# Seven half-size block products in place of eight in a dense expert's first GEMM, one batch at a time

## The chip, the cores and the metric

The kernel runs on one core of a Trainium2 chip. The metric is the device time of one execution in microseconds (us). TensorE (PE) multiplies, VectorE (DVE), ScalarE (ACT) and GpSimd (POOL) do the rest, SyncE (SP) issues most transfers. The engines run on their own, each in its own fixed order, and wait for one another by semaphores.

## The reference

Attention whose mask keeps pairs with equal hash codes, then a mixture of 8 dense experts in which every token goes through every expert, then one in which each token goes to 2 of 8 experts. B = 2 batches, H = 8 heads, S = 768, head size 64; N = B S = 1536 tokens, D = 512, F = 1024, E = 8, all in float32.

```
x = attention(q, k, v, proj)                    # N x D
P = exp(x @ w_gate - max)
for _ in range(8):                              # Sinkhorn
    P /= P.sum(1, keepdims=True) + 1e-09
    P /= P.sum(0, keepdims=True) + 1e-09
    P *= N / E
for e in range(E):                              # dense experts
    h = np.maximum(x @ w1[e], 0.0)              # first GEMM,  D -> F
    out += P[:, e:e + 1] * (h @ w2[e])          # second GEMM, F -> D
...
noisy = out @ w_gate2 + log1p(exp(out @ w_noise)) * noise
# top 2 of 8, softmax over the two, then for each expert e and its tokens m:
out2[m] += top2_w[m] * (np.maximum(out[m] @ v1[e], 0.0) @ v2[e])
```

## The kernel before

Every large product is done three times in a reduced float32 format: an operand is split into a high part (a copy that rounds) and a low part (value minus high part), and high·high, high·low and low·high are added in one PSUM bank.

*Attention* (lines 130 to 386). Its steps are issued by a table of times in units of half a head. The last ones of a head pair are the fold steps: POOL adds two halves and writes the high and low parts of x, `xh` and `xl` (L327, L53, L331); the last pair of a batch goes through PE instead (`fold_last`).

*Dense experts* (`moe1`). Sixteen steps u: expert u // 2, half of F u % 2. In each, three tiles t of 512 tokens. For a tile, GEMM1 makes four banks `ph` (128 units of F by 512 tokens) of 4 × 3 matmuls 128x512 (L507 to L509); ACT writes the high part `hh` (relu, L512), DVE the low part `hl` (L513). Then GEMM2 makes four banks `py` (128 tokens by 512) of 4 × 3 matmuls (L520 to L522), and DVE adds them, times the expert's weight, to `acc` (L530). The weights come in pieces of 512x512, 1 MB each (`Pieces.fetch`, L400), and are split in four chunks by ACT (L418) and DVE (L419) a step ahead. Each piece is fetched once.

*Gate and routing.* `moe1_gate` gets the gate's logits in 24 matmuls and runs Sinkhorn (a chain of small DVE operations with one small matmul each round, L481) while the first dense step runs. In the last dense step, as each token tile of `acc` is finished, `Route.tile` writes it out and transposes it, and `Route.span` computes the choice for some tiles together (`SPANS`), with a PE chain of its own (L593, L594, L599).

*Sparse experts* (`moe2_round`). 416 slots for each expert, filled by a gather (L755) and transposed by PE (L767). The first expert takes its tokens in two units of `CAPH` = 256 slots: its first `JH` = 5 token tiles, whose gather starts before the dense stage ends, and the rest.

*What sets the order.* A scheduler orders the instructions of each engine ahead of time from its own model of durations, under the program's data dependencies, pool sizes and priorities. PSUM has 8 banks: three for `ph`, three for `py`, two for small things (`PsPools`). The instructions of GEMM1 (L507 on) are put by it into the attention's tail where x is ready.

Of the kernel before, what the change touches and what calls it, by code (L numbers as in the profile page):

```python
# [18 lines left out]
P = 128  # L19
NC = S // P           # query/key tiles per batch  # L20
NJ = B * NC           # token tiles
N = B * S
# [10 lines left out]
assert CAP + 4 * CAP2 == N and 0 <= 2 * CAPH - CAP <= CAPH and JH in SPANS  # L33


# when the steps of the attention are issued, in halves of a head
# [5 lines left out]
SUMS = [1.52, 2.12, 2.38, 1.85, 2.31, 2.53]  # L42
EARLY = [4, 7, 9, "g", "g", "g"]
WARM = [26, -0.0, 10]
FIRST = [27.07, 27.44, 27.71, 31.92]
# [10 lines left out]
def build_consts(nc, pool, tmp, proj):  # L56
# [13 lines left out]
    # routing tables  # L70
# [10 lines left out]
    # a token's row in the scratch, 128 j + p, and in the output  # L81
# [8 lines left out]
def attention_consts(nc, pool, c):  # L90
    # [I; I] placed in columns 0..63 or 64..127
# [9 lines left out]
    # what 0 counts as in each row of the codes, and the rows' scale  # L101
# [14 lines left out]
def projections(nc, c):  # L116
    """High and low parts, of a head pair, negated and as they are: columns 0..11 and 32..43 for queries, 64 more for keys."""
# [12 lines left out]
def attention(ctx, tc, c, q, k, v, xh, xl, others=()):  # L130
# [40 lines left out]
    def split_half(st, nm, hf):  # L171
        """High and low parts, transposed; the queries times -1/8."""
# [12 lines left out]
    def stack(st, nm):  # L185
        """One product has high and low queries over high keys twice, the other high queries over low keys, and the codes."""
# [4 lines left out]
        if nm == "q":  # L191
            # [hi0 lo0] [hi1 lo1]; [hi0 .] [hi1 .]
# [5 lines left out]
        else:  # L198
            # [hi0 hi0] [hi1 hi1]; [lo0 .] [lo1 .]
# [24 lines left out]
            # 1 where positive, else -1: 0 is not positive  # L224
# [26 lines left out]
    # ---- per half of a head: 3 query tiles  # L251
    def score(st, x, hf, i, un):
# [5 lines left out]
        if st.first and x == 0:  # L258
            # its parts as they are, before any move
# [9 lines left out]
        # the scores are negated  # L269
# [6 lines left out]
    def norm(un):  # L276
        """e / (sum + 1e-9), or 1 / S in a row without a matching key."""
# [44 lines left out]
    def fold(st, hf, step):  # L322
        """The products with the high values and those with the low ones, added; a pair of heads stacked."""
        xs = slice(st.b * S + hf * 384, st.b * S + hf * 384 + 384)
        a, b = (t[:, cols(hf)] for t in st.ab)
        if step == 0:
            tc.keep_in_program_order(nc.gpsimd.tensor_add(a, a, b))  # L327
        elif step == 1:
            copy_on_pool(nc, xh[:, st.pair, xs], a)
        else:  # L330
            tc.keep_in_program_order(nc.gpsimd.tensor_sub(xl[:, st.pair, xs], a, xh[:, st.pair, xs].bitcast(F32)))  # L331

    def fold_last(st, hf):
        xs = slice(st.b * S + hf * 384, st.b * S + hf * 384 + 384)
# [4 lines left out]
        nc.scalar.activation(xh[:, st.pair, xs], px, AF.Copy)  # L339
        nc.vector.tensor_sub(xl[:, st.pair, xs], px, xh[:, st.pair, xs].bitcast(F32))  # L340
# [3 lines left out]
    for m in range(B * H // 2):  # L344
# [36 lines left out]
        else:  # L381
            for hf in range(2):
                for i in range(3):
                    at(t0 + 3 + VALUE[-1] + 0.01 + SUMS[3 * hf + i], fold, st, hf, i)
# [5 lines left out]
class Pieces:  # L390
    """The weights as 512 x 512 pieces, loaded and split into high and low parts ahead of use."""

    def __init__(self, nc, rawpool, pools, srcs):
        self.nc, self.rawpool, self.pools, self.srcs = nc, rawpool, pools, srcs
        self.raw, self.part = {}, {}

    def fetch(self, i):
        if i < len(self.srcs) and i not in self.raw:
            r = self.rawpool.tile([P, 4, FH], F32, name="wraw", tag="wraw")
            self.nc.sync.dma_start(r, self.srcs[i][0].rearrange("(c p) f -> p c f", p=P))  # L400
            self.raw[i] = r

    def chunk(self, i, k):
        return (slice(None), slice(None), slice(k * P, (k + 1) * P)) if self.srcs[i][1] else (slice(None), k)

    def high(self, i):
# [590 lines left out]
```

## Time and profile before

| | |
|---|---|
| median of 3 runs | 1736.48 us (1736.42 to 1738.51) |
| profiled execution, span | 1738.8 us |
| instructions | 21681 |
| PE busy | 1699.5 us (98%) |
| DVE busy | 770.6 us (44%) |
| ACT busy | 559.3 us (32%) |
| POOL busy | 267.7 us (15%) |

The profiled execution's own time is its span, from the first to the last instruction; no other time of it is recorded. It lies 2.3 us above the median of the runs. The attention takes about the first 290 us, the dense experts go to about 1374, the sparse ones to the end. Busy time counts an engine while it works on an instruction; matmuls overlap in PE's pipeline, so the distance between two starts says what one of them costs, and its own duration is longer.

### The profile page before, as it was taken

Reading aid. Unit: us, or ns where it says so; the run is one execution under the profiler, and the core shown is the slowest. Engines: PE = TensorE matmul, PEld = TensorE weight load, DVE = VectorE, ACT = ScalarE, POOL = GpSimd, SP = SyncE. Lnnn points to the kernel's source line nnn. Section 1 sums busy time; section 2 is a strip of 40 time slices with the busy share of each in tenths; the row PEclk is TensorE's granted clock in tenths of the full one; section 3 lists DMA queues with packets and bytes.
Section 4 is the critical chain, followed back from the end, with each engine's and each line's share of the span. In section 5 each row is a group of like instructions: output and inputs, shape, how many; then the busy total and the mean of one; then the engine's idle time right before and its main releaser. Section 6 shows DMA issues by size and latency. Waiting matters only on the chain. (4 is left out here: it accounts for less than half of the span.)

```text
span 1738.8 us, 21681 instructions
## 1 busy us (share of the span) xinstructions
PE 1699.5 (98%) x8504; PEld 1451.1 (83%) x8504; DVE 770.6 (44%) x1611; ACT 559.3 (32%) x1129; POOL 267.7 (15%) x282
## 2 busy tenths in 40 slices
PE   9999999999999999999999999999999999999995
PEld 6988897788888888888888888888888899999995
DVE  4998995353233233333332333332333765443340
ACT  3878884322021121121121121121111344444431
POOL 3676762002000000000000000000000022322221
PEclk7999999999999999999999999999999999999997
DMA  6755421211010010010010010110101235555531
GB/s 144 193 137 135 96 68 27 75 47 33 16 49 25 25 49 25 25 49 25 25 49 25 25 49 5 45 49 1 49 25 67 92 94 155 156 149 140 145 89 22
DMA packets 87581, 117.21 MB, mean 67 GB/s; under 512 B 33784, under 2 KB 41976, under 8 KB 87472
## 3 DMA queue, kind: packets, MB, share of 16 engines
q1 hardware_dynamic: 80240, 101.60, 19.9%
q0 software_dynamic: 7232, 14.15, 4.4%
q8 instruction: 69, 1.13, 0.3%
q14 instruction: 40, 0.33, 0.1%
HBM read 83.77 MB, written 13.35 MB: 56 GB/s over the span
## 5 line engine op out<-in xcount | busy, mean ns | idle before, releaser
L512 ACT ACTIVATE hh<-ph 128x512 fp32r<-128x512 f32 x192 | 114.0, 596 | 753.0 <-PE ph L509 753.0
L509 PE MATMUL ph<-xh,wlo 128*128 128x512 f32 x768 | 303.6, 395 | 0.0
L508 PE MATMUL ph<-xl,whi 128*128 128x512 f32 x768 | 303.1, 395 | 0.0
L507 PE MATMUL ph<-xh,whi 128*128 128x512 f32 x768 | 302.1, 394 | 0.0
L521 PE MATMUL py<-wlo,hh 128*128 128x512 f32 x768 | 296.1, 395 | 0.0
L520 PE MATMUL py<-whi,hh 128*128 128x512 f32 x768 | 292.0, 396 | 0.0
L522 PE MATMUL py<-whi,hl 128*128 128x512 f32 x768 | 288.9, 395 | 0.0
L513 DVE SCALAR_TENSOR_TENSOR hl<-ph,hh 128x512 fp32r<-128x512 f32 x192 | 132.4, 691 | 326.0 <-ACT hh L512 326.0
L530 DVE SCALAR_TENSOR_TENSOR acc<-py,Pm,acc 128x512 f32<-128x512 f32 x168 | 121.2, 748 | 296.2 <-PE py L522 296.1
L419 DVE TENSOR_TENSOR wlo<-wraw,whi 128x512 fp32r<-128x512 f32 x252 | 159.0, 688 | 109.1 <-ACT whi L418 106.7
L755 POOL DMA_INDIRECT xg<-x2d,idx x32 | 35.3, 1104 | 1013.4 <-DVE idx L751 949.1
L418 ACT ACTIVATE whi<-wraw 128x512 fp32r<-128x512 f32 x252 | 138.4, 620 | 126.3 <-PE py L522 32.2
L507 PEld LDWEIGHTS ph<-xh,whi 128*128 128x128 f32 x768 | 144.9, 189 | 33.8 <-ACT e L272 0.2
L520 PEld LDWEIGHTS py<-whi,hh 128*128 128x128 f32 x768 | 144.3, 188 | 34.4
L522 PEld LDWEIGHTS py<-whi,hl 128*128 128x128 f32 x768 | 144.2, 188 | 34.4
L521 PEld LDWEIGHTS py<-wlo,hh 128*128 128x128 f32 x768 | 144.2, 188 | 34.3
L508 PEld LDWEIGHTS ph<-xl,whi 128*128 128x128 f32 x768 | 144.2, 188 | 33.4
L509 PEld LDWEIGHTS ph<-xh,wlo 128*128 128x128 f32 x768 | 144.2, 188 | 33.1
L294 DVE TENSOR_TENSOR el<-pe,eh 128x384 fp32r<-128x384 f32 x192 | 101.0, 548 | 12.5 <-ACT eh L293 12.1
L285 POOL TENSOR_SCALAR e<-e,f,g 128x768 f32<-128x768 f32 x96 | 93.3, 985 | 54.8 <-DVE f L283 45.7
L290 PE MATMUL pe<-ident,e 128*128 128x128 f32 x576 | 93.5, 275 | 6.3 <-DVE el L294 5.2
L270 DVE TENSOR_REDUCE mn<-pS 128x1 f32<-128x768 f32 x96 | 91.1, 949 | 18.0 <-PE pS L268 18.0
(253 smaller groups left out, 2367.1 us busy)
## 6 DMA issues: line engine op xcount, KB each, us to landing
wraw<-in_moe_w_dram SPq DMA_DIRECT2D x64, 1024.0 KB
ab<-pvf SPq DMA_DIRECT2D x28, 192.0 KB
raw_q<-in_q_dram SPq DMA_DIRECT2D x16, 192.0 KB
raw_k<-in_k_dram SPq DMA_DIRECT2D x16, 192.0 KB
raw_v<-in_v_dram SPq DMA_DIRECT2D x8, 384.0 KB
ka<-kh SPq DMA_DIRECT2D x16, 192.0 KB
out_dram<-zero SPq DMA_DIRECT2D x1, 3072.0 KB
x2d<-acc SPq DMA_DIRECT2D x12, 256.0 KB
```

What stands on the lines that cost most here:

```text
L294: nc.vector.tensor_sub(el, pt, eh.bitcast(F32))
L418: nc.scalar.activation(hi[ix], r[ix], AF.Copy)
L419: nc.vector.tensor_sub(lo[ix], r[ix], hi[ix].bitcast(F32))
L507: nc.tensor.matmul(ph, w1h[:, k, fs], xh[:, k, ts], start=(k == 0), stop=False)
L508: nc.tensor.matmul(ph, w1h[:, k, fs], xl[:, k, ts], start=False, stop=False)
L509: nc.tensor.matmul(ph, w1l[:, k, fs], xh[:, k, ts], start=False, stop=(k == DC - 1))
L512: nc.scalar.activation(hh, ph, AF.Relu)
L513: nc.vector.scalar_tensor_tensor(hl, ph, 0.0, hh.bitcast(F32), op0=ALU.max, op1=ALU.subtract)
L520: nc.tensor.matmul(py, a, w2h[:, k, :], start=(k == 0), stop=False)
L521: nc.tensor.matmul(py, a, w2l[:, k, :], start=False, stop=False)
L522: nc.tensor.matmul(py, b, w2h[:, k, :], start=False, stop=(k == 3))
L530: nc.vector.scalar_tensor_tensor(acc[:, j, :], py, Pm[:, j, e:e + 1], acc[:, j, :], op0=ALU.mult, op1=ALU.add)
```

## The change

The dense stage takes one batch (768 tokens) at a time, in 32 steps n: batch n // 16, expert, half of F. In a step, GEMM1 is x (768 x 512) times w1 (512 x 512). Both are cut into 2 x 2 blocks (384 tokens by 256 of D; 256 of D by 256 of F), and the four result blocks are made from seven products of sums of blocks (Winograd's form of Strassen's scheme) in place of eight products of blocks. The sums of x's blocks are made once per batch (`left`), those of w1's blocks once per step, on POOL (`source`), and split into high and low parts as all operands are (`right`). A product is 2 × 2 × 3 matmuls 128x384, 84 in a step. Four of the seven add to a bank that holds an earlier product. The sums over products are taken from PSUM by ACT and DVE (`hidden`); then GEMM2 goes over the batch's six token tiles (`output`), its matmuls as before, 72 in a step.

Around it: the weights are fetched for either batch, in pieces of half a MB and chunks of 128 rows; the folds of the attention write x itself, in float32 (one POOL addition); gate and routing use 48 float32 matmuls each, straight from x, in place of split operands; routing takes three token tiles together and does batch 0 in the middle of the stage; JH is 6 and CAPH 224; PSUM has four banks for GEMM1 and two for GEMM2.

```diff
-JH, CAPH = 5, 256
-SPANS = {2: 0, 5: 2, 9: 5, 12: 9}
+JH, CAPH = 6, 224
+HT = S // 2
+FP = F // 4
...
-            copy_on_pool(nc, xh[:, st.pair, xs], a)
-            tc.keep_in_program_order(nc.gpsimd.tensor_sub(xl[:, st.pair, xs], a, xh[:, st.pair, xs].bitcast(F32)))
+        tc.keep_in_program_order(nc.gpsimd.tensor_add(xr[st.b][:, st.pair, cols(hf)], a, b))
...
+        src = self.srcs[key].rearrange("(h c p) f -> h p c f", p=P, c=2)
+        for h in range(2):
+            r = self.rawpool.tile([P, 2, FH], F32, name="wraw", tag="wraw")
+            self.nc.sync.dma_start(r, src[h])
...
+    for j in range(NJ):
         for k in range(DC):
-            nc.tensor.matmul(pg, wga[:, 0, k, :], xh[:, k, ts], start=(k == 0), stop=False)
-            nc.tensor.matmul(pg, wga[:, 1, k, :], xl[:, k, ts], start=False, stop=(k == DC - 1))
+            nc.tensor.matmul(pl[:, j], xr[j // NC][:, k, (j % NC) * P:(j % NC + 1) * P], wg[:, k], start=(k == 0), stop=(k == DC - 1))
...
+class Dense:
+    def source(self, n, i):
...
+        if i in (0, 2, 6):
+            return (b11, b21, b22)[i // 2 if i < 6 else 2]
+        def t(m, x, y):
...
+                nc.gpsimd.tensor_sub(o, x, y)
...
+        t1 = t(1, b12, b11)
+        if i == 4:
+            return t1
+        if i == 3:
+            return t(3, b22, b12)
+        t2 = t(2, b22, t1)
+        return t2 if i == 1 else t(4, b21, t2)
+    def right(self, n, i, on_pool=False):
...
+            nc.scalar.activation(hi, src, AF.Copy)
+            nc.vector.tensor_sub(lo, src, hi.bitcast(F32))
+    def left(self, b, xo, tmp):
...
+            nc.vector.tensor_add(s[0], x21[:, k], x22[:, k])
+            nc.vector.tensor_sub(s[1], s[0], x11[:, k])
+            nc.gpsimd.tensor_sub(s[2], x11[:, k], x21[:, k])
+            nc.gpsimd.tensor_sub(s[3], x12[:, k], s[1])
...
+    def hidden(self, n, hp, tmp, after):
...
+        for i in range(7):
+            at = "xyxyzyz"[i]
...
+                for k in range(2):
+                    nc.tensor.matmul(ph, wh[:, k, fs], xh[:, k], start=(i in (0, 1, 4) and k == 0), stop=False, skip_group_check=True)
+                    nc.tensor.matmul(ph, wh[:, k, fs], xl[:, k], start=False, stop=False, skip_group_check=True)
+                    nc.tensor.matmul(ph, wl[:, k, fs], xh[:, k], start=False, stop=(k == 1), skip_group_check=True)
+            for s in range(2):
+                ph, su = banks[s][at], sums[s]
+                if i == 0:
...
+                    nc.scalar.activation(su["p1"], ph, AF.Copy)
+                elif i in (1, 3):
...
+                    nc.vector.tensor_add(su[i], ph, su["p1"])
+                elif i == 2:
+                    keep(s, 0, 0, ph)
+                else:
+                    v, (t, f) = {4: (su[3], (1, 1)), 5: (su["p1"], (1, 0)), 6: (su[1], (0, 1))}[i]
+                    nc.vector.tensor_add(v, ph, v)
+                    keep(s, t, f, v)
...
-    for u in range(2 * E):
+    dense.left(0, xo, tmp)
+    for n in range(steps):
...
+            if i < 4:
+                wt.split(w2(n), i)
+            if i == 1:
+                wt.fetch(w1(n + 1))
...
+        dense.hidden(n, hp, tmp, after)
+        if n == 0:
+            moe1_gate(nc, c, gp, ps, wg, xr, Pm)
+        if last and b == 0:
+            dense.left(1, xo, tmp)
+        for m in range(6):
+            t, i = 1 - m // 3, m % 3
+            j, a = dense.output(n, t, i, acc, Pm)
...
+            if n + 1 < steps:
+                dense.right(n + 1, m)
...
-                      for t, b in (("h", 3), ("y", 3), ("g", 2))}
+                      for t, b in (("h", 4), ("y", 2), ("g", 2))}
```

`keep` takes relu's high part on ACT and its low part on DVE. Line numbers of the kernel after are its own.

PE's order at the end of the attention, before: the last scores (`pS`) and transposes (`pe`), and behind them GEMM1 (`ph`).

```order
L268 MATMUL pS<-kb,qb 128x384
L290 MATMUL pe<-ident,e 128x128 x15
L507 MATMUL ph<-xh,whi 128x512
L508 MATMUL ph<-xl,whi 128x512
L509 MATMUL ph<-xh,wlo_3522 128x512
```

After, at the end of the attention; `px` of L330 and L331 is the last fold, `px` and `py` of L561 on are banks of products 0 and 1.

```order
L330 MATMUL px<-pvs,fold 128x384
L331 MATMUL px<-pvs,fold 128x384
L561 MATMUL px<-xh_4143,wh 128x384 x2
L561 MATMUL py<-xh_4145,wh 128x384 x2
L562 MATMUL px<-xl_4144,wh 128x384
L563 MATMUL px<-xh_4143,wl 128x384
```

The first matmuls of GEMM1 stand between the attention's last transposes before, and behind its last fold after.

DVE's order in the middle of a dense step, before: low parts of hidden units (`hl`), of weights (`wlo`), and accumulations (`acc`).

```order
L513 SCALAR_TENSOR_TENSOR hl_7420<-ph_7406,hh_7419 128x512
L513 SCALAR_TENSOR_TENSOR hl_7437<-ph_7423,hh_7436 128x512
L419 TENSOR_TENSOR wlo_7638<-wraw_7251,whi_7637 128x4x128 x4
L513 SCALAR_TENSOR_TENSOR hl_7454<-ph_7440,hh_7453 128x512
L530 SCALAR_TENSOR_TENSOR acc_4164<-py_7457,Pm_4171,acc_4164 128x512
```

After, in a step, from product 4 on: sums over a bank (`u`, `p1`), low parts of hidden units (`hl`), of w2 (`wl` of L412) and of w1's blocks of the next step (`wl` of L506).

```order
L576 TENSOR_TENSOR u_6159<-pz_6167,u_6159 128x384
L576 TENSOR_TENSOR u_6161<-pz_6174,u_6161 128x384
L412 TENSOR_TENSOR wl_6428<-wraw_6357,wh_6427 128x512
L576 TENSOR_TENSOR p1_6089<-py_6097,p1_6089 128x384
L548 SCALAR_TENSOR_TENSOR hl_6183<-u_6159,hh_6182 128x384
L548 SCALAR_TENSOR_TENSOR hl_6188<-u_6161,hh_6187 128x384
L576 TENSOR_TENSOR p1_6091<-py_6104,p1_6091 128x384
L412 TENSOR_TENSOR wl_6448<-wraw_6357,wh_6447 128x512
L576 TENSOR_TENSOR u_6111<-pz_6167,u_6111 128x384
L548 SCALAR_TENSOR_TENSOR hl_6205<-p1_6089,hh_6204 128x384
L576 TENSOR_TENSOR u_6113<-pz_6174,u_6113 128x384
L506 TENSOR_TENSOR wl_6594<-wt_6591,wh_6593 128x512
```

A bank now passes through a sum before its parts are taken, and a weight's low part stands between the sums.

## Rows read from the trace of the kernel before

**Rows 1.** The page: busy time of each engine; PE's granted clock in 40 slices

```profile
PE 1699.5 (98%) x8504; PEld 1451.1 (83%) x8504; DVE 770.6 (44%) x1611; ACT 559.3 (32%) x1129; POOL 267.7 (15%) x282
...
PEclk7999999999999999999999999999999999999997
```

**Rows 2.** Stretches of the dense stage: busy time (instructions) of engines, clock, DMA

```profile
480.00:680.00 200.00, 200.00 (x860) 161.36 (x860) 64.14 (x96) 33.21 (x59) 0.00 (x0) 1.00 0.10 32
...
1080.00:1280.00 200.00, 200.00 (x861) 161.61 (x860) 64.71 (x96) 33.98 (x60) 0.00 (x0) 1.00 0.10 32
```

**Rows 3.** PE in time: start, duration, line, operation; 384 columns wide

```profile
273.13 0.33 PE L302 MATMUL pv<-eh,vv 128*128 128x384 f32 x1
...
275.03 0.34 PE L303 MATMUL pv<-el,vv 128*128 128x384 f32 x1
```

**Rows 4.** PE in time, sparse stage, 416 columns wide

```profile
1441.09 0.35 PE L841 MATMUL ph<-exh,whi 128*128 128x416 f32 x1
...
1447.52 0.35 PE L842 MATMUL ph<-exl,whi 128*128 128x416 f32 x1
```

**Rows 5.** Groups: busy time, mean ns of one, and idle time before

```profile
L419 DVE TENSOR_TENSOR wlo<-wraw,whi 128x512 fp32r<-128x512 f32 x252 | 159.0, 688 | 109.1 <-ACT whi L418 106.7 <-PE ph L509 2.4
...
L418 ACT ACTIVATE whi<-wraw 128x512 fp32r<-128x512 f32 x252 | 138.4, 620 | 126.3 <-PE py L522 32.2 <-PE ph L508 31.3 <-DMA wraw<-in_moe_w_dram 27.4
L513 DVE SCALAR_TENSOR_TENSOR hl<-ph,hh 128x512 fp32r<-128x512 f32 x192 | 132.4, 691 | 326.0 <-ACT hh L512 326.0
L530 DVE SCALAR_TENSOR_TENSOR acc<-py,Pm,acc 128x512 f32<-128x512 f32 x168 | 121.2, 748 | 296.2 <-PE py L522 296.1
...
L294 DVE TENSOR_TENSOR el<-pe,eh 128x384 fp32r<-128x384 f32 x192 | 101.0, 548 | 12.5 <-ACT eh L293 12.1
...
L293 ACT ACTIVATE eh<-pe 128x384 fp32r<-128x384 f32 x192 | 88.3, 492 | 27.0 <-PE pe L290 19.5 <-PE pv L302 6.7 <-ACT eh L293 0.3
```

**Rows 6.** Groups on POOL

```profile
L430 POOL TENSOR_TENSOR wlo<-wraw,whi 128x512 fp32r<-128x512 f32 x4 | 5.1, 1298 | 0.0
```

**Rows 7.** DVE and POOL in time at 266; all of L294, shortest, median, longest

```profile
266.46 0.97 DVE L281 TENSOR_SCALAR sm<-sm 128x3 f32<-128x3 f32 x1 [0.57 <-ACT e L272]
...
266.40 1.98 POOL L331 TENSOR_TENSOR xl<-ab,xh 128x384 fp32r<-128x384 f32 x2
...
L294 DVE TENSOR_TENSOR el<-pe,eh x192: 521/549/559, 42.1 to 284.4; 128x384 fp32r<-128x384 f32 x192
```

**Rows 8.** PE in time, from the first expert's unit 0 to unit 1

```profile
1404.46 0.60 PE L767 MATMUL pxt<-ident,xg 128*128 128x128 f32 x4
...
1406.82 0.48 PE L841 MATMUL ph<-exh,whi 128*128 128x256 f32 x2
```

**Rows 9.** PE in time, around a Sinkhorn matmul

```profile
387.78 0.28 PE L481 MATMUL pc<-cs,ones 128*128 128x8 f32 x2
387.92 0.48 PE L507 MATMUL ph<-xh,whi 128*128 128x512 f32 x1
388.23 0.39 PE L508 MATMUL ph<-xl,whi 128*128 128x512 f32 x1
```

**Rows 10.** Groups on PE: a small matmul of the routing

```profile
L599 PE MATMUL pl<-fold,lt 32*128 32x16 f32 x24 | 3.3, 261 | 0.5 <-ACT lt L596 0.5
```

**Rows 11.** The end of the attention as one stretch

```profile
260.00:300.00 40.00, 37.66 (x197) 31.50 (x197) 24.57 (x54) 18.91 (x43) 10.77 (x12) 1.00 0.03 3
```

**Rows 12.** PE in time, sparse stage, with the idle time before

```profile
1584.69 0.72 PE L876 MATMUL py<-ehh,whi 128*128 128x416 f32 x1 [2.04 <-ACT ehh L846]
```

**Rows 13.** A stretch of the dense stage with one weight piece's transfer

```profile
565.00:572.00 7.00, 7.00 (x31) 5.65 (x31) 1.77 (x3) 1.20 (x2) 0.00 (x0) 1.00 0.51 150
```

**Rows 14.** PE in time at two waits, and the stretch behind them

```profile
1373.84 1.06 PE L599 MATMUL pl<-fold,lt 32*128 32x16 f32 x8 [0.51 <-ACT lt L596]
...
1376.18 0.94 PE L767 MATMUL pxt<-ident,xg 128*128 128x128 f32 x4 [0.70 <-DVE d L610]
...
1376.00:1380.00 4.00, 3.82 (x15) 3.67 (x16) 3.04 (x15) 0.85 (x3) 0.00 (x0) 0.57 0.64 245
```

More of the change, by code (lines that the diff above doesn't have):

```diff
@@ L127, in projections, with attention @@
             nc.vector.tensor_copy(c.hw[nm][hs, :, at:at + 12], p2[hs].bitcast(F32))
-def attention(ctx, tc, c, q, k, v, xh, xl, others=()):
+def attention(ctx, tc, c, q, k, v, xr, others=()):
     nc = tc.nc
@@ L382, in attention @@
             for hf in range(2):
-                for i in range(3):
-                    at(t0 + 3 + VALUE[-1] + 0.01 + SUMS[3 * hf + i], fold, st, hf, i)
+                at(t0 + 3 + VALUE[-1] + 0.01 + SUMS[hf], fold, st, hf)
     for _, _, fn, a in sorted(steps, key=lambda s_: s_[:2]):
@@ L489, in moe1 @@
+def moe1(ctx, tc, c, dense, wt, ps, wg, xa, xr, route, first, ep):
     nc = tc.nc
-    hp = ctx.enter_context(tc.tile_pool(name="m_h", bufs=6, side="right"))
-    gp = ctx.enter_context(tc.tile_pool(name="m_g", bufs=1, side="right"))
+    xo = ctx.enter_context(tc.tile_pool(name="xo", bufs=1, side="right", reuse_waits="tile"))
+    tmp = ctx.enter_context(tc.tile_pool(name="m_t", bufs=6, side="right", reuse_waits="tile"))
+    hp = ctx.enter_context(tc.tile_pool(name="m_h", bufs=8, side="right", reuse_waits="tile"))
+    gp = ctx.enter_context(tc.tile_pool(name="m_g", bufs=1, side="right", reuse_waits="tile"))
@@ new lines, in moe1, with w1, w2, after @@
+    steps = 4 * E
+    def w1(n):
+        return "w1", n // 2 % E, n % 2, n // (2 * E)
+    def w2(n):
+        return "w2", n // 2 % E, n % 2, n // (2 * E)
+    dense.left(0, xo, tmp)
+    for i in range(3, 7):
+        dense.right(0, i)
+    for n in range(steps):
+        b, u = n // (2 * E), n % (2 * E)
+        wt.fetch(w2(n))
+        def after(i):
+            if i < 4:
+                wt.split(w2(n), i)
+            if i == 1:
+                wt.fetch(w1(n + 1))
+            if n == steps - 1 and i > 2:
+                wt.split(("v1", 0, 0), i - 3, i < 6)
+        dense.hidden(n, hp, tmp, after)
+        if n == 0:
+            moe1_gate(nc, c, gp, ps, wg, xr, Pm)
+        if u == 0:
+            acc = xa.tile([P, NC, D], F32, name="acc", tag="xa")
+        last = u == 2 * E - 1
+        if last and b == 0:
[3 more added lines that the diff above has]
+            j, a = dense.output(n, t, i, acc, Pm)
+            if last:
+                route.tile(j, a, b)
+                if i == 2:
+                    route.span(j - 2, j + 1)
+            if n + 1 < steps:
+                dense.right(n + 1, m)
+                if m == 5:
+                    dense.right(n + 1, 6)
+            elif m < 4:
+                wt.split(("v1", 0, 1), m)
+            else:
+                wt.split(("v2", 0, 0), 2 * m - 8)
+                wt.split(("v2", 0, 0), 2 * m - 7)
+            if n == steps - 1 and m == 0:
+                first.tokens(nc, c, ep, ps, CAPH, "g")
+        if last and b == 0:
+            route.first_half("g")
+        if n == steps - 3:
+            first.gather(nc, c, ep, ps, route.x2d[0:JH * P, :], route.rka, None, "g")
@@ L804, in tokens, with key, piece @@
         return units[n].tokens(nc, c, xp, ps, cap, "gh")
+    def key(e, x):
+        return ("v1", "v2")[x // 2], e, x % 2
+    def piece(e, x):
+        for k in range(4):
+            wt.split(key(e, x), k, x == 0 and k < 3)
     if first:
@@ L810, in moe2_round @@
     if not first:
-        for i in range(2):
-            pc.split(p0 + i)
+        for x in range(2):
+            piece(0, x)
         table(0)
@@ L907, in lsh_moe_kernel @@
-    pc = Pieces(nc, rawpool, [const0, None], dense() + sparse())
+    rawpool = ctx.enter_context(tc.tile_pool(name="wraw", bufs=4))
+    tpool = ctx.enter_context(tc.tile_pool(name="wt", bufs=3))
+    few = ctx.enter_context(tc.tile_pool(name="w0", bufs=3))
+    wt = Weights(nc, rawpool, few, None)
+    def sparse():
+        wt.srcs.update({(x, e, h): w[e][:, h * FH:(h + 1) * FH] if x == "v1" else w[e][h * FH:(h + 1) * FH, :]
+                        for x, w in (("v1", w12), ("v2", w22)) for e in range(E) for h in range(2)})
@@ L908, in lsh_moe_kernel @@
+    sparse()
+    wt.srcs.update({(x, e, h, b): w[e][:, h * FH:(h + 1) * FH] if x == "w1" else w[e][h * FH:(h + 1) * FH, :]
+                    for x, w in (("w1", w1), ("w2", w2)) for e in range(E) for h in range(2) for b in range(B)})
     with ExitStack() as c1:
-        xp = c1.enter_context(tc.tile_pool(name="x", bufs=1, side="right"))
-        xh = xp.tile([P, DC, N], F32R, name="xh")
-        xl = xp.tile([P, DC, N], F32R, name="xl")
+        xa = c1.enter_context(tc.tile_pool(name="x", bufs=2, side="right"))
+        xr = [xa.tile([P, DC, S], F32, name="xr", tag="xa") for _ in range(B)]
+        dense = Dense(nc, c, None, wt, tpool, xr)
@@ L946, in lsh_moe_kernel @@
         with ExitStack() as c5:
-            moe2_round(c5, tc, c, Pieces(nc, rawpool, pc.pools, sparse()), 0, ps, rt, x2d, out, CAP2, None, "1")
+            again = Weights(nc, rawpool, few, wt.many)
+            again.srcs = wt.srcs
+            moe2_round(c5, tc, c, again, ps, rt, x2d, out, CAP2, None, "1")
             nc.vector.tensor_single_scalar(rt.rk, rt.rk, -float(CAP2), op=ALU.add)
```

365 lines of the change are left out of this document (170 added, 195 removed).

## Prediction

> **What bounds the kernel now.** I read the page's first two parts first: TensorE's matmuls (PE) cover 98% of the span, VectorE (DVE) 44%, and the clock row stands at 9 in every slice but the first and the last [rows 1]. An average over four stages proves little, so I cut the dense experts out by stretches: from 480 to 1280 PE is busy for 200.00 us in each 200, DVE for 64 to 65, ScalarE (ACT) for 33 to 34, GpSimd (POOL) for none, at a clock of 1.00 [rows 2]. PE waits for nothing there. So the matmuls' own time is the time, and what is taken from it comes back whole as long as the others keep up. I work from the span of the profiled execution, 1738.8 us; the median of the three runs, 1736.48, is 2.3 below it, and the sum gets these 2.3 off at its end.
>
> **The change part by part.**
>
> *GEMM1.* Rows on PE overlap, so a matmul's price is the distance between starts. For 512 columns: 860 or 861 matmuls in each 200 us, 3443 in all [rows 2], 800 / 3443 = 0.2324 us. For 384: 11 distances from 273.13 to 275.03, 0.1727 [rows 3]. For 416: 34 from 1441.09 to 1447.52, 0.1891 [rows 4]. Per column that is 0.454, 0.450 and 0.455 ns: the price goes with the columns, and smaller matmuls lose nothing. 384 / 512 × 0.2324 = 0.1743. Before, 16 half experts × 3 tiles × 4 × 4 × 3 = 2304 matmuls: 535.4 us. After, 32 steps (a batch and half an expert) × 7 products × 2 × 2 × 3 = 2688 of 384 columns: 468.5. **−66.9**; with 0.1727 it is −71.2, with 0.1765 (1% above 0.1743, more than the three prices differ per column) −61.0. GEMM2 keeps its 2304 matmuls of 512.
>
> *What a step asks of the others.* A step's PE work is 84 × 0.1743 + 72 × 0.2324 = 31.4 us. DVE gets low parts of 7 weight blocks and of 4 pieces of w2 (11 × 0.688), 10 sums over a PSUM bank (the nearest row is el, 0.548), 8 low parts of 384 columns (0.548), 6 accumulations (0.748) [rows 5]: 7.57 + 5.48 + 4.38 + 4.49 = 21.9 us, 70% of the step, where it was 32%. ACT: 11 × 0.620 + 10 × 0.492 = 11.7. POOL, idle there before, gets 4 differences of weight blocks, each like its 128x512 subtraction of 1.298 [rows 6]: 5.2 us. No engine becomes the bound by its sum. What can show is the order. In DVE's rows of the change the sums of products 4, 5 and 6 and their low parts follow one another, with a weight's low part in between. GEMM2's first output needs the low part of product 5's first half; from the end of that half PE still has the second half and product 6, 18 × 0.1743 = 3.1 us, while DVE's sum, ACT's relu, DVE's low part and a weight's low part in front take 0.548 + 0.492 + 0.548 + 0.688 = 2.3. Some 0.8 us are to spare: a usual step waits for nothing, a few slip. I take 0.3 us a step for 30 steps, **+9**, with ends 0 (no wait, as before) and +32 (1 us a step); below nothing it can't be, since nothing is taken from PE by it.
>
> *The same 4 differences* put POOL and DVE side by side, which the dense stage never had. Where they met before, at 266.46, a DVE operation on 128x3 elements, SBUF in and out, took 0.97 us under POOL's subtractions from 266.40 on, while el, which reads PSUM and SBUF, kept to 521 to 559 ns in all its 192 [rows 7]. [...] In the rows' own terms DVE with 21.9 + 5.2 = 27.1 us still fits into 31.4, but 0.8 us to spare is less than one 1.298.
>
> *First expert.* Two units of 224 slots for two of 256: 2 × 192 matmuls × 32 columns × 0.454 ns = −5.6. But unit 0's matmuls also cover the gather and transposition for unit 1: the last transposes start at 1404.46, unit 1's first matmul at 1406.82 [rows 8], right behind. Half of the 5.6 is unit 0's and shortens this cover. Ends −5.6 and 0; I take **−2.8**.
>
> *Gate.* 24 matmuls of 512 (5.6 us) and 12 small transposes (about 1) go; 48 small float32 matmuls come. In the Sinkhorn loop, one with 8 columns (two records) starts 0.14 us before the next dense matmul and 0.45 before the one behind that [rows 9]; 0.45 less 0.2324 is 0.22. 48 × 0.22 = 10.6, less 6.6: +4. At the 0.14 they cost 6.7: about 0. I take **+3**.
>
> *Routing.* Gate matmuls of 12,288 columns (5.6 us) and 12 small ones go, the latter at 0.261 a record, of which two overlap [rows 10], so 3; 48 float32 matmuls of 16 columns come, 6.7 to 12: −2 to +3.4, **+2**.
>
> *The end of the attention.* From 260 to 300 PE idles for only 2.34 of 40 us [rows 11], because GEMM1's first matmuls (59 before 294, 13.7 us) fill the holes, as PE's order shows. After, GEMM1 begins behind the last fold and then needs block sums of x and their parts, 15 operations on DVE (12 of 384 columns at 0.548, 3 of 768 at twice that: 9.9 us), of which the first product needs only its own; the gate's matmuls can fill some of it. Ends 0 and +15; **+7**, the middle.
>
> *Elsewhere.* The Sinkhorn chain, before hidden behind a DVE with room, now queues in steps 1 and 2 with the rest: 0 to +6, **+3**. At the change of batch, routing and the second set of block sums go into two steps that leave DVE 9.5 us each: 0 to +10, **+3**. In the sparse stage weights come in halves, and the one long wait there, 2.04 at 1584.69 [rows 12], may shrink, with the slow matmuls behind it: −4 to 0, **−2**. The weights of the dense stage are fetched twice: its DMA share of 0.10 [rows 2] becomes 0.20, no bound. SP's queue holds nothing else in a steady step, and a block is asked for behind product 1 and first read some five products (10 us) later; a piece of 1 MB went through within 7 us, 150 GB/s × 7 us [rows 13]. [...]
>
> *Sum.* −66.9 − 2.8 + 3 + 2 + 7 + 3 + 3 + 9 − 2 = −44.7; 1738.8 − 44.7 = 1694.1, and 2.3 off: **1692 us**. With the steady term at 0 to 15 and half of the ramps' spread, the case runs from 1676 to 1706.
>
> **The rivals.**
> 1. *All new work is hidden.* For it: PE waited for nothing in 800 us, and DVE keeps 9.5 us free in each step. The steady +9 goes, and of the ramps' 13 some 4 to 6 stay: 1670 to 1676. Against it: the tail loses its filler with certainty.
> 2. *DVE and POOL collide in each step.* A wait of 0.5 (1.298 less the 0.8 to spare) to 1.3 us × 32 = 16 to 42 in place of the 9: with the ramps as forecast 1699 to 1725; from 1706 on I count it here, and with long ramps it reaches 1740; its middle is 1715. For it: 266.46, and that the differences are issued when the next weights arrive, just where products 4 to 6 run. Against it: the sums over PSUM are like el, which never slowed.
> [...]
> 4. *Not seven products.* PE's order has 84 matmuls of 384 in a step, 7 × 12; so I give it none.
>
> **How the numbers follow.** Forecast (1676 to 1706) 0.60; all hidden 0.15; collisions 0.16; the clock 0.07; below 1670, 0.02. A measurement of this kernel tells 0.2% (3.5 us) from no change. Of the collisions 0.03 end within that and 0.01 above; so faster 0.89, within 0.03, slower 0.08. The range for 8 in 10 is 1670 to 1722: outside are the collisions' upper part (0.06), the clock (0.07) and the low end (0.02), some 0.15, and I leave the last 0.05 for what no row shows.
>
> **What would show it.** Right: in a steady step 384-wide matmuls 0.174 apart, about 31.7 us from one step to the next, DVE near 70%, a clock of 1.00, and PE idle for some 7 us between the attention's last products and the second step. Collisions: low parts of weights with a mean well above 0.688 and a largest near 2 us, and waits of PE for the low parts of products 5 or 6 in most steps. The clock: digits below 9 in the middle slices. The forecast is wrong if a step takes 33 us or more, if 384-wide matmuls stand more than 0.177 apart without a wait, or if the gate, the routing or the ramps cost over 30 us together.

## The result and the profile after

The changed kernel takes 1690.49 us (median of 4 runs, 1688.83 to 1694.35), the kernel before beside it 1736.45 (1735.48 to 1738.51): a ratio of 0.974, interval [0.9725, 0.9755]. Forecast was 1692. In a second series, beside the last experiments, it took 1693.08 (0.9773 [0.9745, 0.9801]).

First the page of the changed kernel, its busy times and PE's granted clock in 40 slices, which answer [rows 1]:

```profile
span 1687.1 us, 24582 instructions
PE 1642.6 (97%) x8991; PEld 1498.9 (89%) x8991; DVE 1161.1 (69%) x2224; ACT 755.1 (45%) x1497; POOL 445.9 (26%) x382
...
PEclk8999998999999999999999999999999999999998
```

PE's busy time fell by 57 us and its share hardly, so it is still the bound. The clock row has an 8 in its seventh slice, 253 to 295 us, where the dense stage begins. DVE's share went from 44 to 69%, POOL's from 15 to 26. A stretch of steady steps, as in [rows 2] (length, then busy time and count of PE, PE's weight loads, DVE, ACT, POOL, then clock, DMA share and GB/s):

```profile
860.00:1080.00 220.00, 220.00 (x1092) 197.32 (x1091) 159.97 (x249) 80.28 (x148) 41.73 (x29) 1.00 0.23 68
```

PE is busy for all of it, with DVE at 160 / 220 = 73% (70 forecast). The length of a step stands between the first matmuls of two steps (PE in time: start, duration, line, operation):

```profile
923.80 0.35 PE L561 MATMUL px<-xh,wh 128*128 128x384 f32 x1
...
955.32 0.34 PE L561 MATMUL px<-xh,wh 128*128 128x384 f32 x1
```

That is 31.5; most of the 32 steps take 31.45 to 31.52 (31.46 below), where the matmuls' price without a wait was 31.37 (31.4 in the prediction). To find the rest, the time is cut at two places that both kernels have: the last fold of the attention and the first matmul of the sparse stage. Those of the kernel before:

```profile
293.87 0.34 PE L338 MATMUL px<-pvs,fold 128*128 128x384 f32 x1
...
1379.62 0.36 PE L841 MATMUL ph<-exh,whi 128*128 128x256 f32 x1
```

of the changed one:

```profile
272.62 0.52 PE L331 MATMUL px<-pvs,fold 128*128 128x384 f32 x1
...
1326.67 0.35 PE L962 MATMUL ph<-exh,wh 128*128 128x224 f32 x1
```

From the 293.87 come off 14.4 for the matmuls of GEMM1 that stood in the attention then (62 at 0.2324; the prediction counted 59), and they go to the dense stage.

| stage, us | before | after | after, run again |
|---|---|---|---|
| attention | 279.5 | 272.6 | 277.2 |
| dense | 1100.2 | 1054.1 | 1053.7 |
| of it the dense steps' matmuls | 4608 × 0.2324 = 1070.9 | 32 × 31.46 = 1006.7 | 1006.7 |
| of it all else | 29.3 | 47.4 | 47.0 |
| sparse | 359.2 | 360.4 | 358.9 |
| span | 1738.8 | 1687.1 | 1689.8 |

The attention's 4.6 us between two executions of the same kernel come from its start: the stretch from 20 to 40 us in the changed kernel's trace, and in that of its second execution.

```profile
20.00:40.00 20.00, 19.66 (x73) 14.48 (x74) 9.67 (x21) 9.30 (x21) 8.18 (x11) 0.74 0.65 133
```

```profile
20.00:40.00 20.00, 20.00 (x51) 13.54 (x50) 5.93 (x14) 6.73 (x15) 4.28 (x6) 0.50 0.62 126
```

The granted clock is 0.74 in one and 0.50 in the other, and a third less work is done. The kernel before had 0.50 there too. From 60 us on the second execution is 5.4 us behind, at the attention's end 4.4 to 4.6. Such a start alone lets single runs differ by some 5 us, so the experiments are read by stages and by steps where they can be.

### The profile page after: what moved, and what is told of

Its sections match the earlier page's. It is cut to its first block, busy times and chain, and to the rows that moved or that the text cites. A ratio compares the mean times of both kernels' runs of the same rounds, so it can differ in the third digit from the quotient of the medians.

```text
span 1687.1 us, 24582 instructions
## 1 busy us (share of the span) xinstructions
PE 1642.6 (97%) x8991; PEld 1498.9 (89%) x8991; DVE 1161.1 (69%) x2224; ACT 755.1 (45%) x1497; POOL 445.9 (26%) x382
## 5 line engine op out<-in xcount | busy, mean ns | idle before, releaser
L591 PE MATMUL py<-wh,hh 128*128 128x512 f32 x768 | 305.7, 398 | 0.0
L592 PE MATMUL py<-wl,hh 128*128 128x512 f32 x768 | 304.1, 396 | 0.0
L593 PE MATMUL py<-wh,hl 128*128 128x512 f32 x768 | 299.8, 397 | 1.0 <-DVE hl L548 1.0
L412 DVE TENSOR_TENSOR wl<-wraw,wh 128x512 fp32r<-128x512 f32 x256 | 180.4, 734 | 43.3 <-ACT wh L411 42.8
L411 ACT ACTIVATE wh<-wraw 128x512 fp32r<-128x512 f32 x256 | 153.9, 630 | 68.7 <-PE pz L562 30.0
L593 PEld LDWEIGHTS py<-wh,hl 128*128 128x128 f32 x768 | 145.1, 189 | 34.4 <-DVE hl L548 1.8
L592 PEld LDWEIGHTS py<-wl,hh 128*128 128x128 f32 x768 | 145.3, 189 | 28.7
L591 PEld LDWEIGHTS py<-wh,hh 128*128 128x128 f32 x768 | 145.1, 189 | 27.0 <-DVE acc L606 0.2
L562 PE MATMUL py<-xl,wh 128*128 128x384 f32 x384 | 130.4, 340 | 1.7 <-DVE xl L520 1.7
L561 PE MATMUL py<-xh,wh 128*128 128x384 f32 x384 | 130.4, 341 | 1.5 <-DVE u L571 1.5
L506 DVE TENSOR_TENSOR wl<-wt,wh 128x512 fp32r<-128x512 f32 x127 | 87.9, 695 | 30.2 <-ACT wh L505 29.2
L294 DVE TENSOR_TENSOR el<-pe,eh 128x384 fp32r<-128x384 f32 x192 | 101.1, 548 | 6.4 <-ACT eh L293 5.8
```

The lines of the kernel that those rows point to most:

```text
L294: nc.vector.tensor_sub(el, pt, eh.bitcast(F32))
L411: nc.scalar.activation(hi, r, AF.Copy)
L412: nc.vector.tensor_sub(lo, r, hi.bitcast(F32))
L561: nc.tensor.matmul(ph, wh[:, k, fs], xh[:, k], start=(i in (0, 1, 4) and k == 0), stop=False, skip_group_check=True)
L562: nc.tensor.matmul(ph, wh[:, k, fs], xl[:, k], start=False, stop=False, skip_group_check=True)
L591: nc.tensor.matmul(py, hh, w2h, start=(x == order[0]), stop=False)
```

## The experiments

**Eight products in the new structure.** All else of the change stays; a bank takes two products and is evacuated directly.

```diff
-        if i in (0, 2, 6):
-            return (b11, b21, b22)[i // 2 if i < 6 else 2]
+        return (b11, b21, b12, b22)[i]
...
-            at = "xyxyzyz"[i]
+        for g, (t, f) in enumerate(((0, 0), (1, 0), (1, 1), (0, 1))):
...
+            for y in range(2):
+                wh, wl = self.w[n, 2 * f + y]
+                xh, xl = self.x[2 * t + y]
```

> Eight plain block products of 384 columns in place of the seven, in the same structure (one batch at a time, half pieces, same gate, routing and attention); no sums of blocks are made. Theory A (matmul columns are the time of a step): 12 more matmuls of 0.175 us in each of 32 steps, +2.1 us a step, +67 us on 1690.5: about 1757, slower than the kernel before by about 20; a step of 33.6 us. Theory B (the sums, their evacuations and POOL's differences cost time of their own that the seven products only just pay): less than +50, under 1740.

1749.83 us (ratio to before 1.0088 [1.0066, 1.011]). A step takes 33.54 us, +2.08, as theory A has it to 0.02. But its dense stage, 1108.8 us, has only 1108.8 − 32 × 33.54 = 35.5 us of other things, 11.5 less than the changed kernel. So seven products for eight bring 66.6 us in the steps and cost 11.5 at their ends. Theory B was wrong on the steps and right that not all is gain: the whole is +59.3 us, between the two theories. Without the scheme the new structure is 15 us slower than the kernel before (1734.61 beside it).

**POOL's differences left out.**

```diff
-                nc.gpsimd.tensor_sub(o, x, y)
-                self.t[n, m] = o
+                self.t[n, m] = x
```

> Left out: POOL's differences of weight blocks in the dense stage (a block itself is split in the place of the difference). Everything else as in the changed kernel. Theory A (POOL's subtractions stop low parts on VectorE that read SBUF twice, but TensorE has the next step's products to go on with): the low parts that now take up to 1.65 us go back to 0.55, and the time stays within 3 us of the changed kernel's 1690.5. Theory B (the collisions are part of the time): 16 us faster or more.

1683.06 us, 7.4 below the changed kernel, between the two theories. The steady step is 31.46 as before; the 9.2 us that its dense stage is shorter lie in the first six steps (4.3) and at the change of batch (4.7). The collisions are there in the changed kernel nonetheless. DVE in time, and POOL in the same stretch of a steady step:

```profile
921.70 3.23 DVE L548 SCALAR_TENSOR_TENSOR hl<-u,hh 128x384 fp32r<-128x384 f32 x2
924.86 0.54 DVE L576 TENSOR_TENSOR p<-py,p 128x384 f32<-128x384 f32 x1
...
928.39 2.11 DVE L548 SCALAR_TENSOR_TENSOR hl<-u,hh 128x384 fp32r<-128x384 f32 x2
```

```profile
921.65 1.29 POOL L483 TENSOR_TENSOR wt<-wraw,wt 128x512 f32<-128x512 f32 x1 [16.71 <-DMA wraw<-in_moe_w_dram]
922.90 1.61 POOL L483 TENSOR_TENSOR wt<-wraw 128x512 f32<-128x512 f32 x1
928.54 1.54 POOL L483 TENSOR_TENSOR wt<-wraw,wt 128x512 f32<-128x512 f32 x1 [4.03 <-DVE wl L506]
```

Two low parts that take 0.55 each alone take 3.23 and 2.11 together under POOL's subtractions, which take up to 1.61 there in place of 1.29. Who was held went by who began first. From 860 to 1280, 47 of the 56 low parts `hl<-u` overlap a difference. 29 of them take 1.18 to 1.66, and each of these began after the difference. The other 18 take 0.54 to 0.55; 17 of them began first, and where they overlapped for long it was the difference that took longer, 1.53 to 2.61 in place of 1.29; the eighteenth came right behind one of these, beside the same difference of 2.61. The 19 sums over PSUM (L576) beside a difference there take 0.54 to 0.55, as those without one do. With the differences left out, nearly all low parts go back to 0.55 (median 555 ns). What the collisions cost DVE stands in ten steady steps (314.6 us, DVE is the third busy time), in the changed kernel and without the differences:

```profile
890.00:1204.60 314.60, 314.60 (x1561) 282.26 (x1560) 231.40 (x350) 114.52 (x210) 58.08 (x40) 1.00 0.23 67
```

```profile
890.00:1204.60 314.60, 314.60 (x1562) 282.44 (x1561) 201.86 (x350) 114.71 (x210) 0.00 (x0) 1.00 0.22 68
```

The same 350 operations take 29.5 us less, so a step's collisions cost DVE 2.9 us, and PE is busy throughout in both.

**The differences twice, and four times.**

```diff
                 nc.gpsimd.tensor_sub(o, x, y)
+                nc.gpsimd.tensor_sub(o, x, y)
```

> Each of POOL's differences of weight blocks is computed twice, so POOL works about 11 us in a step of 31.46 instead of 5.5. Theory A (stopped, but covered): VectorE's time in a step rises by about 1 us more, TensorE does not wait, the time rises by less than 6 us. Theory B (each collision in the wrong place makes TensorE wait, the spare is 0.8 us): 0.5 to 1.3 us in most steps, +16 to +42.

> Each of POOL's differences of weight blocks is computed four times: POOL has 4 x 4 x 1.3 = 21 us in a step, still less than the step's 31.46. Were the engines independent, nothing would change (within 6 us). If POOL and those operations of VectorE that read SBUF twice (11 us of low parts of weights and 3 of hidden units) exclude one another, their 35 us no longer fit into 31.46: every step gets longer by 2 us or more, +60 us or more, and TensorE waits for low parts, with its clock falling behind the waits.

Twice: 1711.03 us (0.9871 [0.9849, 0.9892]), +20.5. Steady steps take 31.62 to 32.95, 32.0 on average: 0.5 a step, 17 us of it. So the cover ends between one and two; theory B's lower end. Four times: 1746.67, +56, but the steps average 32.03, +0.57, no more than with two, and the rest (some 38 us) is in the ramps. The expectation's arithmetic was off: operations of DVE that read SBUF twice are 11 × 0.688 + 6 × 0.548 = 10.9 us in a step, not 14, and with 4 × 4 × 1.29 = 20.6 that is 31.5, just the step. What four differences in a row do to one low part stands in DVE's durations there (shortest, median, longest ns):

```profile
L549 DVE SCALAR_TENSOR_TENSOR hl<-u,hh x128: 543/1635/8284, 304.5 to 1363.5; 128x384 fp32r<-128x384 f32 x128
L549 DVE SCALAR_TENSOR_TENSOR hl<-px,hh x64: 506/545/558, 293.0 to 1348.1; 128x384 fp32r<-128x384 f32 x64
```

The first form reads SBUF twice and was held for up to 8.28 us (906.12 to 914.41, beside six subtractions in a row); the second, the same operation with one input in PSUM, never.

**The differences on DVE.**

```diff
-                nc.gpsimd.tensor_sub(o, x, y)
+                (nc.gpsimd if n == 0 else nc.vector).tensor_sub(o, x, y)
```

> The differences of weight blocks are computed on VectorE in place of POOL from the second step on. VectorE then has 21.9 + 4 x 0.69 = 24.7 us of work in a step of 31.46, POOL none, and no collisions. Theory A (a step's time is TensorE's, the rest is covered either way): within 3 us of the changed kernel's 1690.5. Theory B (the collisions cost more than 2.8 us of VectorE's time do): faster by 10 us or more. Theory C (VectorE at 79% is too full, TensorE waits): slower by 10 us or more.

1694.2 us (1691.46 to 1698.12), 3.7 above the changed kernel and 1.1 above its second series. The steady step is 31.45, the longest `hl<-u` 559 ns, the dense stage 1055.2. By the first series that is just outside theory A's 3 us, by the second within them, and by the steps it is theory A: to a step of PE's length it is all the same where the differences are made.

**TensorE in program order.**

```diff
-                    nc.tensor.matmul(ph, wh[:, k, fs], xh[:, k], ...
+                    self.keep(nc.tensor.matmul(ph, wh[:, k, fs], xh[:, k], ...
...
-            nc.tensor.matmul(py, hh, w2h, start=(x == order[0]), stop=False)
+            self.keep(nc.tensor.matmul(py, hh, w2h, start=(x == order[0]), stop=False))
...
+    dense.keep = tc.keep_in_program_order
```

> TensorE's dense matmuls are kept in the order in which the program is written: no products of the next step between the second GEMM's outputs. Theory A (what hides the late low parts is that TensorE has the next step's products to go on with): in most steps a wait of 0.5 to 1.5 us before the first output, with a lower clock behind it in some, +20 to +60 us. Theory B (the 0.8 us to spare after product 5 are enough by themselves): less than +6 us.

1812.74 us, +122. PE's waits from 480 to 780, and the first of them in time:

```profile
PE py L593 <- DVE hl L548: 11.4, 9, 1.3
```

```profile
573.17 0.50 PE L593 MATMUL py<-wh,hl 128*128 128x512 f32 x1 [1.27 <-DVE hl L548]
```

One wait of 1.27 in each step, always for the low part of product 5, and a step of 32.97: +1.5, 45 us in 30 steps, as theory A has it. (The other 77 are the first step, 81 us long, and the change of batch, where PE can't go past the Sinkhorn's and the routing's results.) DVE at the same place shows why no time was to spare:

```profile
568.35 1.66 DVE L548 SCALAR_TENSOR_TENSOR hl<-u,hh 128x384 fp32r<-128x384 f32 x1
569.93 0.54 DVE L576 TENSOR_TENSOR p<-py,p 128x384 f32<-128x384 f32 x1
570.40 1.18 DVE L548 SCALAR_TENSOR_TENSOR hl<-u,hh 128x384 fp32r<-128x384 f32 x1
571.50 0.54 DVE L576 TENSOR_TENSOR p<-py,p 128x384 f32<-128x384 f32 x1
571.97 0.67 DVE L412 TENSOR_TENSOR wl<-wraw,wh 128x512 fp32r<-128x512 f32 x1
572.57 0.54 DVE L548 SCALAR_TENSOR_TENSOR hl<-p,hh 128x384 fp32r<-128x384 f32 x1
```

The matmuls of product 5's first half end at 568.27, its low part (the last row) at 573.11: 4.84 us, where the prediction had 2.3. The prediction counted the first sum (569.93), one weight's low part and the low part itself. DVE does besides, in this stretch, both low parts of product 4 and the sum of the second half, and the two low parts take 1.66 and 1.18, as those that began after a difference do in the changed kernel (1.18 to 1.66). PE has other work until 571.90, and waits. Had they taken 0.55 each, the low part would have come some 0.5 us before PE needs it; that is an estimate from these rows, and program order without the differences was not run.

In the changed kernel the scheduler had put the next step's first products there (here product 0, `px`), as PE shows at the place:

```profile
924.86 0.40 PE L591 MATMUL py<-wh,hh 128*128 128x512 f32 x1
...
925.79 0.34 PE L561 MATMUL px<-xh,wh 128*128 128x384 f32 x1
...
926.84 0.40 PE L593 MATMUL py<-wh,hl 128*128 128x512 f32 x1
```

And the clock, in the stretch with nine such waits:

```profile
480.00:780.00 300.00, 288.57 (x1420) 256.21 (x1419) 208.36 (x317) 103.65 (x189) 54.79 (x36) 1.00 0.21 64
```

11.4 us of idle time, 1.27 in each step, and the granted clock stays at 1.00. The expected lower clock behind the waits did not come.

**The gate.** Three quarters of its matmuls left out:

```diff
-            nc.tensor.matmul(pl[:, j], ..., start=(k == 0), stop=(k == DC - 1))
+            if k == 0:
+                nc.tensor.matmul(pl[:, j], ..., start=True, stop=True)
```

> Left out: three quarters of the dense gate's float32 matmuls (12 in place of 48). Theory A (each costs 0.215 us of TensorE and nothing else): 36 x 0.215 = 7.7 us faster. Theory B (they stand in time in which TensorE would have waited for block sums): 0 to 3 us faster. Theory C (the runs of 18 and 24 small matmuls also let the granted clock fall, and 5 to 8 us are lost to the lower clock behind them): 11 to 16 us faster, and a granted clock near 1 from 280 to 310 where it is 0.66 and 0.83.

1681.19 us, −9.3 (0.968 [0.9646, 0.9714]); its dense stage is 1041.9, 12.2 less. By the time that is between A and C, by the stage within C. The stretch from 280 to 290 of the changed kernel, and of this one:

```profile
280.00:290.00 10.00, 10.00 (x48) 10.00 (x48) 9.46 (x14) 3.72 (x7) 3.20 (x2) 0.66 0.22 61
```

```profile
280.00:290.00 10.00, 6.71 (x35) 5.59 (x33) 10.00 (x18) 3.98 (x8) 3.03 (x2) 1.00 0.22 61
```

With the gate PE is busy throughout at a clock of 0.66, without most of it PE idles for 3.29 of 10 us at 1.00: the gate fills waits, and slows what follows. What follows, in the changed kernel:

```profile
280.92 2.70 PE L429 MATMUL pl<-wg,xr 128*128 128x8 f32 x18
...
283.94 0.52 PE L562 MATMUL px<-xl,wh 128*128 128x384 f32 x1
284.26 0.52 PE L563 MATMUL px<-xh,wl 128*128 128x384 f32 x1
```

Two experiments set this apart from waits: 24 small matmuls added to each of eight steady steps, in a row or spread.

```diff
+        def small():
+            if left[0]:
+                left[0] -= 1
+                keep_(nc.tensor.matmul(pd[:, left[0] % NJ], self.c.ones, self.c.ones[:, 0:E], start=True, stop=True))
...
+        for _ in range(24):
+            small()
```

So in a row, ahead of the products. Spread, the last two lines go and one stands behind each triple of the products' matmuls. In both, the products of these steps are kept in program order too (`keep_`).

```diff
+                    small()
```

> In eight steady steps (6 to 13) 24 additional float32 matmuls with 8 columns, whose result is not used, stand in a row before the products. Theory A (0.215 us each and nothing else): 24 x 0.215 = 5.2 us in each of these steps, 36.6 us a step. Theory C (a row of small matmuls lets the granted clock fall, though TensorE is never idle): 2 to 4 us more, 38.6 us a step or longer, with 384-wide matmuls 0.32 apart behind the row.

> The same 24 additional small matmuls in the same eight steps, one behind each triple of the products' matmuls in place of a row. Theory A: again 36.6 us a step. Theory C (only a row of them lets the clock fall): 36.6 us a step here, with a granted clock of 1.00 throughout, and 2 us or more less than with the row.

Each ran once, with eight such steps in it. In a row: steps of 40.6 to 41.6 us. Spread: 37.05, so 5.6 / 24 = 0.23 each. The row costs 4.1 us a step more, the same matmuls notwithstanding. A step with the row, and with them spread, as stretches:

```profile
525.00:567.00 42.00, 41.19 (x209) 37.26 (x208) 23.13 (x35) 11.51 (x21) 6.02 (x4) 0.92 0.16 51
```

```profile
525.00:567.00 42.00, 42.00 (x233) 37.93 (x231) 25.84 (x41) 14.59 (x26) 5.68 (x4) 1.00 0.16 51
```

Clock 0.92 and 1.00; by estimate (1 − 0.92) × 42 = 3.4 us for it, and 0.8 of waiting. Theory C, at or above the upper end of what was expected.

**The gate spread.** Two of its matmuls behind each triple of step 0, whose products are then kept in program order:

```diff
+                    if gate:
+                        gate()
```

> The dense gate's 48 small matmuls are put two at a time between the triples of the first step's dense matmuls, in place of runs of 18 and 24. The same work. Theory C (runs of small matmuls let the granted clock fall): 4 to 8 us faster than 1690.5, granted clock above 0.9 in the stretches from 270 to 310. Theory A (the small matmuls cost their 0.215 us each and nothing more; the clock falls for the waits): within 2 us.

The clock is 1.00 in all four stretches from 270 to 310, as theory C has it. The time is not: 1713.14 us, with runs from 1689.32 to 1715.72. In the trace (span 1697.3, dense stage 1057.3) PE now waits 5.2 us once (396.4 to 401.6) for an accumulation that needs the Sinkhorn's result, and the clock is 0.54 from 401 to 408; what was won by the clock was lost there. Four of its six runs lie near 1714. The record has each run's granted clock over the whole span: 0.969 to 0.975 in these four, 0.983 in the traced run, 0.989 in the one of 1689.32. A difference of 0.011 over 1700 us is by estimate 19 us of work at a clock of 1.00, enough for the whole difference, but at which place in the kernel it is lost no trace shows.

**The sparse stage.** PE's waits there, in the changed kernel:

```profile
PE pxt L881 <- DMA xg<-x2d,idx: 4.9, 6, 1.3
```

```diff
-                if nxt:
-                    tokens(m + 1)
+            if d == 3 and nxt:
+                tokens(m + 1)
```

> In the sparse stage the next expert's tokens are transposed before the last of the four output tiles in place of the third, about 4.5 us later in TensorE's order, so that their gathers have landed. Theory A (the 448 slots in place of 512 saved 5.6 us, but six waits for gathers, 4.9 us, took them back): 4 to 6 us faster than the changed kernel. Theory B (the waits move to the next unit's first matmuls, which need the transposed tokens): no faster, within 2 us.

1692.58 us, with the changed kernel at 1693.08 on the same chip: theory B's number, but not its reason. The waits for gathers are still 5.3 us in five: in the first unit that the edit changes, the scheduler moved nine of sixteen transposes and left seven in place, and the waits stand at those. Whether later transposes would help was therefore not tried.

> The changed kernel as it is, beside the others on one chip. 1690.5 within 4 us. If the first 40 us differ between executions (granted clock of 0.50 from 20 to 40 in the trace before, 0.74 in the trace after), its attention ends some 5 us later than 272.6 in an execution with the lower clock.

1693.08 us, within the 4; its attention ends at 277.2 with a clock of 0.50, 4.6 later than 272.6.

No version tried that computes all of the reference is measurably faster than the changed kernel.

## Why the prediction was right, and where only its sum was

*GEMM1's price, −66.9:* right. A step of 31.46 is 84 × 0.175 + 72 × 0.233, and one product more or less is 2.08 us (12 × 0.173).

*Steady waits, +9:* too large. A step has 0.09 over its 31.37, 2.7 us in all. The 0.8 us to spare behind product 5 is what failed. I had DVE's order in front of me, and counted one weight's low part between the sum and the low part where it has four operations more; and I priced none of them as held. In program order the low part comes after 4.84 us in place of 2.3, 1.27 too late, so nothing was to spare. In the changed kernel it comes after 5.0 to 6.2 us (420 to 770; 3.3 to 4.5 with the differences left out), and yet no steady step waits. What covers it are 12 to 24 matmuls of the next step's first products, 2.1 to 4.2 us of work, that the scheduler put between the second GEMM's first outputs. I read DVE's order for this, and not PE's at the same place. That so little is waited for was thus not forecast for its reason.

The collision of rival 2 happens in each step, as its rows [rows 7] suggested, and costs DVE 2.9 us in each; PE doesn't see it. Half of that rival's signs came: low parts are held, those of hidden units above all (of the weights' 13 of the 19 beside a difference, up to 1.78 us); waits of PE in most steps did not. Low parts with two inputs in SBUF were held, up to 8.28 us with four differences; low parts with one in PSUM never (at most 558 ns there), nor the sums over PSUM beside a difference (0.54 to 0.55); and the 17 low parts of hidden units that began before a difference took their 0.55.

*The slower rival, the clock:* it did not come. That each step's wait would have a low clock behind it was my estimate from one place, the wait of 0.70 with 0.57 behind it [rows 14]. Nine waits of 1.27, one in each step, left the clock at 1.00. With a row of 24 small matmuls ahead of a step it was 0.92 over 42 us, PE busy for 41.19 of them, and with the same 24 spread 1.00. The slow stretch 1376 to 1380 stood behind small matmuls too (L599, eight of 16 columns) as well as behind waits of 0.51 and 0.70; which of these did it there is not shown. A longer wait was followed by a fall (2.83 us, and 0.50 behind it, in the last section), but no steady step has one.

*Ramps, gate and routing, +18 in all:* measured +18.1 (47.4 − 29.3; 17.7 in the second trace), by other parts than I had, and they are no sum. The gate's own matmuls take 10.7 us by the distance to the next start, less the 6.6 that I had for what they replaced: +4.1, not +3. From 270 to 310, PE idles for 2.0 us, not 7, and the clock, 0.83, 0.66, 0.83 and 0.83 in the four stretches of 10 us, costs by estimate ((1 − clock) × 10) 1.7 + 3.4 + 1.7 + 1.7 = 8.5, of which 0.7 is in the 10.7. The first 1.7 is not the gate's: the clock falls at 271.9 (0.50 from 272 to 275), ahead of the gate's first matmul at 277.19, and it is 0.83 from 270 to 280 with three quarters of the gate left out, too. The change of batch is two steps of 45.58 and 33.43, 16.1 over two steady ones, of which 4.9 are the routing's matmuls and 2.7 transposes; some 8.5 remain, not +3. There DVE is busy for 18.77 of 20 us and PE for 16.25, at a clock of 0.85:

```profile
780.00:800.00 20.00, 16.25 (x68) 13.34 (x67) 18.77 (x27) 9.36 (x19) 9.01 (x7) 0.85 0.29 104
```

The routing's matmuls are 4.85 + 5.0 = 9.9 us, of which 1.7 stand behind the cut to the sparse stage, for 10.1 before (7.0 of the gate's, eight of them in the stretch at 0.57 [rows 14], and 3.1 of small ones): about nothing, not +2. The Sinkhorn's chain cost PE no wait.

*First expert and weights in the sparse stage, −4.8:* not there (+1.2 and −0.3 in two traces). The 64 slots fewer are 5.6 us of columns. Six waits for gathers, 4.9 us, ate most of them, where the kernel before had one of 0.2; but they stand at later experts (1449 to 1617), not between the first expert's units, where I had looked for them. Why those gathers come later is not shown. The wait of 2.04 [rows 12] and the slow matmuls behind it (a clock of 0.57 from 1584 to 1588) are gone, as forecast. With all waits, that clock and the routing's 1.7 us counted, 2 to 3 us stay open.

*What the sum left out:* the attention ends 2.3 us earlier at the same start (277.2 against 279.5, one trace each; with the same attention and start, that of program order ends at 277.0, that of the later tokens at 278.4). POOL does one fold operation there where it did three, and PE's waits for `el` fell from 5.2 to 2.4 us; that this is the cause is argued, not shown.

So −57.9 for steps forecast and −64.2 measured, +18 and +17.7 for the ramps, −4.8 and about 0 for the sparse stage, 0 and −2.3 for the attention: −44.7 forecast, −49.0 between the two traces that start with a clock of 0.50, −46.0 between the medians of the first series and −41.2 of the second. GEMM1's price, the source of the gain, was right for its reason. That the whole came out within 2 us is luck beside it: terms that were off by 6, 5 and 2 us cancel in part, and the ramps' +18 is made of other parts.

## What to carry to other kernels

Where one engine is busy for all of a stage, count what it does and multiply by the distance between starts: that part came out to 1%. What the other engines do late is paid only if nothing else is ready, so before a collision or a wait is priced, count all that stands in front of it in the order of the engine that is late, and look in the order of the engine that would wait for what it can go on with. And a structure that repeats is paid for at its ends: the first step, the last and the change between two sets cost 18 us here, more than a quarter of what the steps gained.

## What the runs showed of the hardware that was not expected

A row of 24 matmuls with 8 columns (7.0 us, PE never idle) was followed by 384-wide matmuls at 0.52 a record for 3.4 us, where 0.33 is usual; one of them behind each triple left the clock at 1.00. Here is the row and what follows, PE in time of the kernel with the rows:

```profile
529.56 7.02 PE L549 MATMUL pd<-ones 128*128 128x8 f32 x48
...
537.22 0.52 PE L575 MATMUL px<-xh,wl 128*128 128x384 f32 x1
...
540.03 0.34 PE L575 MATMUL px<-xh,wl 128*128 128x384 f32 x1
```

48 records in 6.87 us are 0.143 each, against 0.107 in a row of the changed kernel at a clock of 1.00 (18 in 1.93 us, 277.19 to 279.12); from the two I estimate that the clock fell within the row. Idle time of 1.27 us in 33, nine times over, or 3.29 in 10 (the gate's stretch above), left it at 1.00. A single longer wait was followed by a fall with no row of small matmuls near (the last two records of 8 columns lie 8 us before): in the kernel with four differences, PE's wait and the stretch behind it.

```profile
410.20 0.44 PE L562 MATMUL pz<-xh,wh 128*128 128x384 f32 x1 [2.83 <-DVE u L577]
...
411.40:414.70 3.30, 3.30 (x9) 2.56 (x9) 3.30 (x8) 0.98 (x2) 3.30 (x4) 0.50 0.24 91
```

The fall at 271.9 in the changed kernel, to 0.50, came behind two waits of 1.17 and 0.58 us, 1 us apart, and the one in the spread gate, 0.54 from 401 to 408, with its wait of 5.2 (396.4 to 401.6). So both idle time and rows of small matmuls went ahead of falls here.

The other thing not expected is that not every overlap of POOL and DVE was held alike. Of the 47 low parts of hidden units that met a subtraction on POOL from 860 to 1280, both with two inputs in SBUF, 29 began later and took 1.18 to 1.66 in place of 0.55; where the subtraction began later for long, it took 1.53 to 2.61 in place of 1.29. With four differences one low part stood beside six subtractions in a row, for 8.28 us.
